# A gated feed-forward kernel: smaller first weight groups in separate buffer slots, a first chunk interleaved by input piece, and warmup matmuls

## The chip, the cores and the metric

The kernel runs on one core of a Trainium2 chip. The time is the device time of one execution in microseconds (us), 319.64 us for the kernel before: the median of 6 runs, which lie between 319.05 and 321.4 us. The profile comes from one more execution, of 319.37 us, whose span from the first to the last instruction is 317.6 us.

A core has five engines with their own instruction streams: TensorE (PE, matrix products; its weight loads are shown as PEld), VectorE (DVE), ScalarE (ACT), GpSimd (POOL) and SyncE (SP). They wait for each other on semaphores. Transfers between memory and the on-chip buffers run on 16 DMA engines; SyncE, ScalarE and GpSimd each issue them on a queue of their own (q1, q10 and q0 in the profile).

## What is computed

With x of 1024 rows (32 x 32) and 1024 columns, and weights in bf16:

```python
B, S, D, F = 32, 32, 1024, 3584
# x: (B, S, D), w_gate and w_up: (D, F), w_down: (F, D)
def reference(x, w_gate, w_up, w_down):
    return (_gelu(x @ w_gate) * (x @ w_up)) @ w_down
```

`_gelu` is the tanh approximation of GELU.

## The kernel before

**Tiling.** The hidden dimension F of 3584 is cut into 28 chunks of 128 (`FM = 28`, index m). The contraction over D = 1024 is cut into 8 slices of 128 (`DK`, index dk), the 1024 rows into two halves of 512 (`NH`, index h). For one chunk PE does 16 matmuls for the gate (called G) and 16 for the up projection (U), each 128x128 weights against 128x512 of x (L259). A chunk fills four PSUM banks of 512 columns: two for G, two for U; `s = m % 2` says which half of the eight banks. PE therefore works on one chunk while ScalarE and VectorE turn the other into a slice of `hT`: Square and Sigmoid on ScalarE (L304, L307), three operations on VectorE (L322, L327, L330), the last of which is D3. PE waits for D3 of chunk m - 2 before it starts chunk m. After all chunks a second stage (L279) multiplies `hT` by the down weights `wd`, 448 matmuls, and copies and stores the result.

**Input.** x must lie with its columns on the partitions. SyncE loads it with four DMA transposes (L212), one for each half of the rows (h) and half of the columns (q2): pieces (0,0), (0,1), (1,0), (1,1), each with a semaphore of its own. Slices dk 0 to 3 need q2 = 0, slices 4 to 7 need q2 = 1.

**Weights.** Gate and up weights come in groups of chunks. `gsizes` is 1, 3, and then 4 six times. Each of `wg` and `wu` has two buffers of 512 columns (four chunks), and group j goes to the start of buffer `j % 2`. Gate groups 0 and 1 are issued by ScalarE (L296), the later ones by SyncE (L223) behind the transposes; all up groups are issued by GpSimd (L200). The second group, on both engines, is held back until the second piece of x has landed:

```python
if j == 1:
    act.wait(Q_X[(0, 1)], ctx.get(("x", 0, 1)))
```

GpSimd has the same two lines. From group 2 on a load waits until PE has finished the first chunk of the group before (G of it on SyncE, U of it on GpSimd): then the buffer's old contents have been used. The down weights, seven groups of four chunks (`issue_wd`, L185), are issued between the others.

**Order on PE.** The order is written out by hand in `prog_pe`: chunk by chunk, in a chunk first all of G and then all of U, in each first h = 0 and then h = 1, with dk innermost. In chunk 0 each matmul waits for its piece of x. As all of G comes before U, the last four G matmuls of chunk 0 need piece (1,1), and the 16 U matmuls stand behind them. PE also waits for the group's gate and up loads before the first matmul of the group.

Of the kernel before, what the change touches and what calls it, by code (L numbers as in the profile page):

```python
# [6 lines left out]
P = 128  # L7
# [81 lines left out]
def bass_standalone__geglu_ffn__sampling_kernel(  # L89
# [13 lines left out]
    DK = D // P  # L103
# [3 lines left out]
    DH = D // 512  # L107
    assert NH == 2 and DH == 2 and DK == 8, "kernel specialised for N=1024, D=1024"

    gsizes = [1, 3]  # L110
    while sum(gsizes) < FM:
        gsizes.append(min(4, FM - sum(gsizes)))
    groups = []
    c = 0
    for gsz in gsizes:
        groups.append((c, gsz))
        c += gsz
    NG = len(groups)
    chunk_group = {}
    for j, (c0, gsz) in enumerate(groups):  # L120
        for i in range(gsz):
            chunk_group[c0 + i] = (j, i)
    NWB = 2

    WDG = 4
# [10 lines left out]
    C_DVE = _Clock("dve")  # L136
    C_POOL = _Clock("pool")
    Q_X = {(h, q2): _Clock(f"x{h}{q2}", 16) for h in range(2) for q2 in range(2)}
    Q_WGA = [_Clock("wga0", 16), _Clock("wga1", 16)]
    Q_WG = [_Clock("wg0", 16), _Clock("wg1", 16)]  # L140
    Q_WU = [_Clock("wu0", 16), _Clock("wu1", 16)]
    Q_WD_SP = _Clock("wd_sp", 16)
    Q_WD_POOL = _Clock("wd_pool", 16)
    Q_OUT = _Clock("out", 16)
    all_clocks = [C_PE, C_ACT, C_DVE, C_POOL, *Q_X.values(), *Q_WGA, *Q_WG, *Q_WU,
                  Q_WD_SP, Q_WD_POOL, Q_OUT]

    ctx = _Ctx()
# [1 line left out]
    with ExitStack() as es:  # L150
# [22 lines left out]
        def u_full(s):  # L173
            return ps[:, 4 * s + 2:4 * s + 4, :].rearrange("p a b -> p (a b)")

        def wslice(r, j):
            c0, gsz = groups[j]
            return r[:, :, c0 * P:(c0 + gsz) * P]

        def issue_wd(ew, eng, mine, upto_chunk, clock, force=False):  # L180
            for k in list(mine):
# [5 lines left out]

        def prog_pool(eng):
            pool = _Eng(ctx, eng, C_POOL)
            wd_mine = [k for k in range(len(wd_groups)) if k % 2 == 1]  # L190
            for j in range(NG):
                buf = j % NWB
                c0, gsz = groups[j]
                if j == 1:
                    pool.wait(Q_X[(0, 1)], ctx.get(("x", 0, 1)))
                if j >= NWB:
                    pc0, _pgsz = groups[j - 1]
                    pool.wait(C_PE, ctx.get(("U", pc0)))
                ctx.set(("wu", j), pool.do(
                    lambda: eng.dma_start(wu_bufs[buf][:, :, 0:gsz * P], wslice(wu_r, j)),  # L200
                    clock=Q_WU[buf]))
                if j >= NWB:
                    issue_wd(pool, eng, wd_mine, groups[j - 1][0], Q_WD_POOL)
            issue_wd(pool, eng, wd_mine, FM, Q_WD_POOL, force=True)
            ctx.set("wd_pool_total", Q_WD_POOL.n)

        def prog_sp(eng):
            sp = _Eng(ctx, eng, None)
            for h in range(NH):
                for q2 in range(2):  # L210
                    ctx.set(("x", h, q2), sp.do(
                        lambda: eng.dma_start_transpose(  # L212
                            xT[:, 4 * q2:4 * q2 + 4, h * 512:(h + 1) * 512],
                            xf[h * 512:(h + 1) * 512, q2 * 512:(q2 + 1) * 512],
                        ), clock=Q_X[(h, q2)]))
            wd_mine = [k for k in range(len(wd_groups)) if k % 2 == 0]
            for j in range(NWB, NG):
                buf = j % NWB
                c0, gsz = groups[j]
                pc0, _pgsz = groups[j - 1]  # L220
                sp.wait(C_PE, ctx.get(("G", pc0)))
                ctx.set(("wg", j), sp.do(
                    lambda: eng.dma_start(wg_bufs[buf][:, :, 0:gsz * P], wslice(wg_r, j)),  # L223
                    clock=Q_WG[buf]))
                issue_wd(sp, eng, wd_mine, pc0, Q_WD_SP)
            issue_wd(sp, eng, wd_mine, FM, Q_WD_SP, force=True)
            ctx.set("wd_sp_total", Q_WD_SP.n)
            last = None
            for tc in range(TC):
                for dh in range(DH):  # L230
                    sp.wait(C_ACT if dh == 0 else C_DVE, ctx.get(("E", tc, dh)))
                    last = sp.do(lambda: eng.dma_start(
                        out_r[:, tc, dh * 512:(dh + 1) * 512],
                        osb[:, tc, dh * 512:(dh + 1) * 512]), clock=Q_OUT)
            sp.wait(Q_OUT, last)

        def prog_pe(eng):
            pe = _Eng(ctx, eng, C_PE)
            for m in range(FM):
                j, fi = chunk_group[m]  # L240
                s = m % 2
                buf = j % NWB
                if fi == 0:
                    if j < NWB:
                        pe.wait(Q_WGA[j], ctx.get(("wg", j)))
                    else:
                        pe.wait(Q_WG[buf], ctx.get(("wg", j)))
                    pe.wait(Q_WU[buf], ctx.get(("wu", j)))
                if m >= 2:
                    pe.wait(C_DVE, ctx.get(("D3", m - 2)))  # L250
                for (key, wbufs, bank0) in (("G", wg_bufs, 4 * s), ("U", wu_bufs, 4 * s + 2)):
                    wb = wbufs[buf]
                    v = None
                    for h in range(NH):
                        for dk in range(DK):
                            if m == 0:
                                pe.wait(Q_X[(h, dk // 4)], ctx.get(("x", h, dk // 4)))
                            last = (dk == DK - 1 and h == NH - 1)
                            v = pe.do(lambda: eng.matmul(  # L259
                                ps[:, bank0 + h, :],  # L260
                                wb[:, dk, fi * P:(fi + 1) * P],
                                xT[:, dk, h * 512:(h + 1) * 512],
                                start=(dk == 0), stop=(dk == DK - 1),
                            ), mark=last)
                    ctx.set((key, m), v)
            pe.wait(C_DVE, ctx.get(("D3", FM - 2)))
            pe.wait(Q_WD_SP, ctx.get("wd_sp_total"))
            pe.wait(Q_WD_POOL, ctx.get("wd_pool_total"))
            for tc in range(TC):
                for dh in range(DH):  # L270
                    b = (tc % 4) * 2 + dh
                    if tc >= 4:
                        pe.wait(C_ACT if dh == 0 else C_DVE, ctx.get(("E", tc - 4, dh)))
                    v = None
                    for m in range(FM):
                        if m == FM - 1:
                            pe.wait(C_DVE, ctx.get(("D3", FM - 1)))
                        last = (m == FM - 1)
                        v = pe.do(lambda: eng.matmul(  # L279
                            ps[:, b, :],  # L280
                            hT[:, m, tc * P:(tc + 1) * P],
                            wd[:, m, dh * 512:(dh + 1) * 512],
                            start=(m == 0), stop=(m == FM - 1),
                        ), mark=last)
                    ctx.set(("O", tc, dh), v)

        def prog_act(eng):
            act = _Eng(ctx, eng, C_ACT)
            act.do(lambda: eng.activation(warm[:, 0:1], const0, ACTF.Sigmoid))  # L289
            for j in range(NWB):  # L290
                buf = j % NWB
                c0, gsz = groups[j]
                if j == 1:
                    act.wait(Q_X[(0, 1)], ctx.get(("x", 0, 1)))
                ctx.set(("wg", j), act.do(
                    lambda: eng.dma_start(wg_bufs[buf][:, :, 0:gsz * P], wslice(wg_r, j)),  # L296
                    clock=Q_WGA[j]))
            for m in range(FM):
                s = m % 2
                tb, ib = t_bufs[m % 2], i_bufs[m % 2]  # L300
                act.wait(C_PE, ctx.get(("G", m)))
                if m >= 2:
                    act.wait(C_DVE, ctx.get(("D2", m - 2)))
                ctx.set(("A1", m), act.do(lambda: eng.activation(  # L304
                    tb[:, :], g_full(s), ACTF.Square, scale=SQ_SCALE)))
                act.wait(C_DVE, ctx.get(("D1", m)))
                ctx.set(("A2", m), act.do(lambda: eng.activation(  # L307
                    tb[:, :], ib[:, :], ACTF.Sigmoid, scale=SIG_SCALE)))
            for tc in range(TC):
                dh = 0  # L310
                b = (tc % 4) * 2 + dh
                act.wait(C_PE, ctx.get(("O", tc, dh)))
                ctx.set(("E", tc, dh), act.do(lambda: eng.activation(  # L313
                    osb[:, tc, dh * 512:(dh + 1) * 512], ps[:, b, :], ACTF.Copy)))
# [74 lines left out]
```

## Time and profile before

| What | Value |
|---|---|
| Time, median of 6 | 319.64 us |
| Span of the profiled run | 317.6 us |
| PE busy | 294.6 us, 93% of the span, 1344 matmuls |
| DVE busy / ACT busy | 34% / 20% |
| First matmul of the kernel starts | 7.85 us |
| First matmul after the last piece of x starts | 24.96 us |
| Second stage starts | 217.99 us |
| Last matmul ends | 314.70 us |
| Landing of x pieces, from issue | 4.2 to 15.6 us |
| Landing of the 768 KB loads: wg / wu | 6.1 / 14.9 us from issue |

How to read it: an engine's busy share says how much of the whole span it worked, not what set the end. The chain of waits does that; it goes back from the last instruction to whatever released each step. Lines of the timeline give the start, the length, the engine, the line of the code, the operation with its output and inputs, and a count; in brackets the idle time before it and the work that ended that. A table of windows gives for each stretch the busy time and the number of instructions of PE, PEld, DVE, ACT and POOL, then the granted clock of TensorE (1.00 is full), the busy share of the DMA engines and the rate in GB/s. A DMA share above 100% means that packets of an engine overlapped in time.

### The profile page before, as it was taken

The page shows a single profiled execution, that of the slowest core. Times are in us where ns is not written, and L with a number is a line of the kernel's source. Part 1 is how long each engine was busy: PE and PEld are TensorE (multiplying, and loading weights), DVE is VectorE, ACT ScalarE, POOL GpSimd, SP SyncE. Part 2 cuts the span into 40 slices and gives each one's busy share as a digit, 9 for nine tenths or more (in the row PEclk, how much of TensorE's full clock was granted, in tenths as well). Part 3 has the DMA queues.
Part 4 walks back from the last instruction along what each step waited for, and adds up shares of the span by engine and source line. Part 5 has one row for each costly group of instructions (what it writes and reads, how often), then busy time and mean ns, then how long its engine had stood idle before and what let it go on. Part 6 is the DMA issues. An engine that isn't in the chain of part 4 may idle for free.

```text
span 317.6 us, 2954 instructions
## 1 busy us (share of the span) xinstructions
PE 294.6 (93%) x1344; PEld 131.9 (42%) x1344; DVE 108.1 (34%) x92; ACT 64.5 (20%) x66; POOL 9.7 (3%) x15
## 2 busy tenths in 40 slices
PE   0608999999999999999999999999999999999996
PEld 0103444444444444444444444444444444444442
DVE  0001554455555445455545545554000000000000
ACT  1002222323322232322233232222000000000000
POOL 1100100100010020000002000000000000000000
PEclk9956999999999999999999999999999999999999
DMA  8950440830380086047007700000010000001000
GB/s 169 252 106 1 130 137 0 290 108 0 107 289 2 0 294 236 1 125 274 0 0 255 277 0 0 2 0 0 17 35 17 17 27 25 17 17 35 17 17 33
DMA packets 23788, 26.40 MB, mean 83 GB/s; under 512 B 9968, under 2 KB 19184, under 8 KB 23776
## 3 DMA queue, kind: packets, MB, share of 16 engines
q1 hardware_dynamic: 18976, 14.68, 15.3%
q0 software_dynamic: 2720, 10.49, 10.5%
q10 hardware_dynamic: 2080, 1.05, 1.4%
q8 instruction: 10, 0.16, 0.2%
q14 instruction: 2, 0.02, 0.0%
HBM read 22.02 MB, written 2.10 MB: 76 GB/s over the span
## 4 chain that ended last, share of the span: by engine, by line
PE 91%; DMA 5%; SPq 3%; DVE 0%; issue 0%
PE ps L259 61%; PE ps L279 30%; DMA xT<-in_x_dram 5%; SPq L212 3%; DVE osb L336 0%
## 5 line engine op out<-in xcount | busy, mean ns | idle before, releaser
L259 PE MATMUL ps<-xT,wg 128*128 128x512 bf16 x448 | 104.5, 387 | 20.0 <-DMA xT<-in_x_dram 12.2
L259 PE MATMUL ps<-xT,wu 128*128 128x512 bf16 x448 | 102.5, 382 | 0.0
L279 PE MATMUL ps<-wd,hT 128*128 128x512 bf16 x448 | 96.9, 379 | 0.0
L259 PEld LDWEIGHTS ps<-xT,wg 128*128 128x128 bf16 x448 | 43.9, 99 | 75.2 <-DMA xT<-in_x_dram 14.3
L259 PEld LDWEIGHTS ps<-xT,wu 128*128 128x128 bf16 x448 | 44.1, 99 | 54.2 <-issue 2.2
L279 PEld LDWEIGHTS ps<-wd,hT 128*128 128x128 bf16 x448 | 43.8, 98 | 52.9
L322 DVE SCALAR_TENSOR_TENSOR ib<-tb,ps 128x1024 f32<-128x1024 f32 x28 | 34.2, 1221 | 80.9 <-ACT tb L304 80.9
L304 ACT ACTIVATE tb<-ps 128x1024 f32<-128x1024 f32 x28 | 28.6, 1023 | 121.4 <-PE ps L259 121.4
L327 DVE TENSOR_TENSOR sb<-tb,ps 128x1024 f32<-128x1024 f32 x28 | 34.2, 1221 | 36.1 <-PE ps L259 36.1
L307 ACT ACTIVATE tb<-ib 128x1024 f32<-128x1024 f32 x28 | 29.6, 1057 | 36.0 <-DVE ib L322 36.0
L336 DVE CAST osb<-ps 128x512 bf16<-128x512 f32 x8 | 5.5, 691 | 89.3 <-PE ps L279 89.3
L330 DVE TENSOR_TENSOR hT<-sb,ps 128x1024 bf16<-128x1024 f32 x28 | 34.2, 1220 | 1.0
L313 ACT ACTIVATE osb<-ps 128x512 bf16<-128x512 f32 x8 | 4.8, 597 | 86.6 <-PE ps L279 86.6
L200 POOL DMA_DIRECT2D wu<-in_w_up_dram x8 | 7.2, 903 | 161.7 <-PE ps L259 153.3
L185 POOL DMA_DIRECT2D wd<-in_w_down_dram x3 | 2.3, 760 | 0.0
L289 ACT ACT_TABLE_LOAD x1 | 1.3, 1283 | 0.7 <-PEq L374 0.7
L289 ACT ACTIVATE warm<-const-float32-0.0 128x1 f32<-128x1 f32 x1 | 0.2, 203 | 0.0
L374 POOL MEMSET const-float32-0.0<- 128x1 f32 x1 | 0.1, 98 | 0.2 <-issue 0.2
L374 POOL MEMSET const-bfloat16-1.0<- 128x1 bf16 x1 | 0.1, 101 | 0.0
L374 POOL MEMSET const-float32-1.0<- 128x1 f32 x1 | 0.1, 98 | 0.0
L374 POOL MEMSET const-uint8-127<- 128x1 uint8 x1 | 0.1, 98 | 0.0
## 6 DMA issues: line engine op xcount, KB each, us to landing
wg<-in_w_gate_dram SPq DMA_DIRECT2D x6, 1024.0 KB, 5.4
wu<-in_w_up_dram POOLq DMA_DIRECT2D x6, 1024.0 KB, 7.2
wd<-in_w_down_dram SPq DMA_DIRECT2D x4, 1024.0 KB, 7.7
wd<-in_w_down_dram POOLq DMA_DIRECT2D x3, 1024.0 KB, 8.3
out_dram<-osb SPq DMA_DIRECT2D x16, 128.0 KB, 1.7
wg<-in_w_gate_dram ACTq DMA_DIRECT2D x1, 768.0 KB, 6.1
wu<-in_w_up_dram POOLq DMA_DIRECT2D x1, 768.0 KB, 14.9
wg<-in_w_gate_dram ACTq DMA_DIRECT2D x1, 256.0 KB, 3.7
```

Of the source, the lines that this page charges most:

```text
L185: ew.do(lambda: eng.dma_start(wd[:, a:b, :], wd_r[:, a:b, :]), clock=clock)
L200: lambda: eng.dma_start(wu_bufs[buf][:, :, 0:gsz * P], wslice(wu_r, j)),
L212: lambda: eng.dma_start_transpose(xT[:, 4 * q2:4 * q2 + 4, h * 512:(h + 1) * 512], xf[h * 512:(h + 1) * 512, q2 * 512:(q2 + 1) * 512],), c ...
L259: v = pe.do(lambda: eng.matmul(ps[:, bank0 + h, :], wb[:, dk, fi * P:(fi + 1) * P], xT[:, dk, h * 512:(h + 1) * 512], start=(dk == 0), sto ...
L279: v = pe.do(lambda: eng.matmul(ps[:, b, :], hT[:, m, tc * P:(tc + 1) * P], wd[:, m, dh * 512:(dh + 1) * 512], start=(m == 0), stop=(m == F ...
L304: ctx.set(("A1", m), act.do(lambda: eng.activation(tb[:, :], g_full(s), ACTF.Square, scale=SQ_SCALE)))
L307: ctx.set(("A2", m), act.do(lambda: eng.activation(tb[:, :], ib[:, :], ACTF.Sigmoid, scale=SIG_SCALE)))
L313: ctx.set(("E", tc, dh), act.do(lambda: eng.activation(osb[:, tc, dh * 512:(dh + 1) * 512], ps[:, b, :], ACTF.Copy)))
L322: ctx.set(("D1", m), dve.do(lambda: eng.scalar_tensor_tensor(out=ib[:, :], in0=tb[:, :], scalar=1.0, in1=g_full(s), op0=ALU.add, op1=ALU.m ...
L327: ctx.set(("D2", m), dve.do(lambda: eng.tensor_tensor(sub[:, :], tb[:, :], u_full(s), ALU.mult)))
L330: ctx.set(("D3", m), dve.do(lambda: eng.tensor_tensor(hT[:, m, :], sub[:, :], g_full(s), ALU.mult)))
L336: ctx.set(("E", tc, dh), dve.do(lambda: eng.tensor_copy(osb[:, tc, dh * 512:(dh + 1) * 512], ps[:, b, :])))
```

## The change

There are three edits, all for the start of the kernel.

1. **Weight groups and slots.** The groups become 1, 1, 2, 3, then 4 five times and a last one of 1. Each group gets a buffer and a first slot in it; groups 2 and 3 are put beside groups 0 and 1 in the same buffers (slots from 1), so that they needn't wait for PE. What a later group must wait for is worked out from the slots' last users (`group_war`). Each group has semaphores of its own. Groups 0 and 1 are issued at once, without waiting for x. On GpSimd, group 2 waits for the second piece of x; SyncE issues gate groups 2 and 3 straight after the transposes. Loads are to be ready earlier.
2. **Chunk 0 by piece of x.** PE goes through chunk 0 in the order of the four pieces, and for each piece does four G and four U matmuls. All other chunks keep their order. More work is to be done as x comes in.
3. **Warmup.** GpSimd fills 128x512 elements of the output buffer with ones as its first instruction, and PE multiplies these eight times into a PSUM bank before its real work. This is to raise PE's clock early.

```diff
-    gsizes = [1, 3]
+    gsizes = [1, 1, 2, 3]
     while sum(gsizes) < FM:
         gsizes.append(min(4, FM - sum(gsizes)))
...
+    for j, gsz in enumerate(gsizes):
+        if j < 4:
+            buf, slot0 = (j % 2), (0 if j < 2 else 1)
+        else:
+            buf, slot0 = (j % 2), 0
+        groups.append((c, gsz, buf, slot0))
...
+    for j, (c0, gsz, buf, slot0) in enumerate(groups):
+        prev = [slot_owner.get((buf, sl)) for sl in range(slot0, slot0 + gsz)]
+        prev = [pp for pp in prev if pp is not None]
+        group_war.append(max(prev) if prev else None)
...
         def prog_pool(eng):
             pool = _Eng(ctx, eng, C_POOL)
+            ctx.set("scr", pool.do(lambda: eng.memset(osb[:, 0, 0:512], 1.0)))
...
-                if j == 1:
+                if j == 2:
                     pool.wait(Q_X[(0, 1)], ctx.get(("x", 0, 1)))
-                if j >= NWB:
-                    pc0, _pgsz = groups[j - 1]
-                    pool.wait(C_PE, ctx.get(("U", pc0)))
+                if group_war[j] is not None:
+                    pool.wait(C_PE, ctx.get(("U", group_war[j])))
...
         def prog_sp(eng):
...
-            for j in range(NWB, NG):
-                pc0, _pgsz = groups[j - 1]
-                sp.wait(C_PE, ctx.get(("G", pc0)))
+            for j in range(2, NG):
+                if group_war[j] is not None:
+                    sp.wait(C_PE, ctx.get(("U", group_war[j])))
...
+        NDUMMY = 8
+
         def prog_pe(eng):
             pe = _Eng(ctx, eng, C_PE)
+            pe.wait(C_POOL, ctx.get("scr"))
+            for i in range(NDUMMY):
+                v = pe.do(lambda: eng.matmul(ps[:, 7, :], osb[:, 0, 0:P], osb[:, 0, 0:512],
+                                             start=True, stop=True), mark=(i == NDUMMY - 1))
+            pe.wait(C_PE, v)
...
+                if m == 0:
+                    order = []
+                    for (h, q2) in XPIECES:
+                        for key in ("G", "U"):
+                            for dk in range(4 * q2, 4 * q2 + 4):
+                                order.append((key, h, dk))
...
         def prog_act(eng):
-            for j in range(NWB):
-                if j == 1:
-                    act.wait(Q_X[(0, 1)], ctx.get(("x", 0, 1)))
+            for j in range(2):
                 ctx.set(("wg", j), act.do(
```

More of the change, by code (lines that the diff above doesn't have):

```diff
@@ L114, in bass_standalone__geglu_ffn__sampling_kernel @@
     c = 0
-    for gsz in gsizes:
-        groups.append((c, gsz))
+    for j, gsz in enumerate(gsizes):
[3 more added lines that the diff above has]
+            buf, slot0 = (j % 2), 0
+        assert slot0 + gsz <= 4
+        groups.append((c, gsz, buf, slot0))
         c += gsz
     NG = len(groups)
-    chunk_group = {}
-    for j, (c0, gsz) in enumerate(groups):
+    chunk_info = {}
+    for j, (c0, gsz, buf, slot0) in enumerate(groups):
         for i in range(gsz):
-            chunk_group[c0 + i] = (j, i)
+            chunk_info[c0 + i] = (j, buf, slot0 + i)
+    group_war = []
+    slot_owner = {}
+    for j, (c0, gsz, buf, slot0) in enumerate(groups):
+        prev = [slot_owner.get((buf, sl)) for sl in range(slot0, slot0 + gsz)]
+        prev = [pp for pp in prev if pp is not None]
+        group_war.append(max(prev) if prev else None)
+        for sl in range(slot0, slot0 + gsz):
+            slot_owner[(buf, sl)] = c0 + gsz - 1
     NWB = 2
@@ L138, in bass_standalone__geglu_ffn__sampling_kernel @@
     Q_X = {(h, q2): _Clock(f"x{h}{q2}", 16) for h in range(2) for q2 in range(2)}
-    Q_WGA = [_Clock("wga0", 16), _Clock("wga1", 16)]
-    Q_WG = [_Clock("wg0", 16), _Clock("wg1", 16)]
-    Q_WU = [_Clock("wu0", 16), _Clock("wu1", 16)]
+    Q_WG = [_Clock(f"wg{j}", 16) for j in range(NG)]
+    Q_WU = [_Clock(f"wu{j}", 16) for j in range(NG)]
     Q_WD_SP = _Clock("wd_sp", 16)
@@ L144, in bass_standalone__geglu_ffn__sampling_kernel @@
     Q_OUT = _Clock("out", 16)
-    all_clocks = [C_PE, C_ACT, C_DVE, C_POOL, *Q_X.values(), *Q_WGA, *Q_WG, *Q_WU,
+    all_clocks = [C_PE, C_ACT, C_DVE, C_POOL, *Q_X.values(), *Q_WG, *Q_WU,
                   Q_WD_SP, Q_WD_POOL, Q_OUT]
@@ L174, in u_full, with wsrc, wdst @@
             return ps[:, 4 * s + 2:4 * s + 4, :].rearrange("p a b -> p (a b)")
-        def wslice(r, j):
-            c0, gsz = groups[j]
+        def wsrc(r, j):
+            c0, gsz, _buf, _slot0 = groups[j]
             return r[:, :, c0 * P:(c0 + gsz) * P]
+        def wdst(bufs, j):
+            _c0, gsz, buf, slot0 = groups[j]
+            return bufs[buf][:, :, slot0 * P:(slot0 + gsz) * P]
         def issue_wd(ew, eng, mine, upto_chunk, clock, force=False):
@@ L189, in prog_pool @@
             pool = _Eng(ctx, eng, C_POOL)
+            ctx.set("scr", pool.do(lambda: eng.memset(osb[:, 0, 0:512], 1.0)))
             wd_mine = [k for k in range(len(wd_groups)) if k % 2 == 1]
+            known_chunk = -1
             for j in range(NG):
-                buf = j % NWB
-                c0, gsz = groups[j]
-                if j == 1:
+                c0, gsz, buf, slot0 = groups[j]
+                if j == 2:
                     pool.wait(Q_X[(0, 1)], ctx.get(("x", 0, 1)))
-                if j >= NWB:
-                    pc0, _pgsz = groups[j - 1]
-                    pool.wait(C_PE, ctx.get(("U", pc0)))
+                if group_war[j] is not None:
+                    pool.wait(C_PE, ctx.get(("U", group_war[j])))
+                    known_chunk = max(known_chunk, group_war[j])
@@ L199, in prog_pool @@
                 ctx.set(("wu", j), pool.do(
[L200 to L203, printed above, removed]
+                    lambda: eng.dma_start(wdst(wu_bufs, j), wsrc(wu_r, j)),
+                    clock=Q_WU[j]))
+                if j >= 2:
+                    issue_wd(pool, eng, wd_mine, known_chunk, Q_WD_POOL)
@@ L204, in prog_pool @@
             issue_wd(pool, eng, wd_mine, FM, Q_WD_POOL, force=True)
             ctx.set("wd_pool_total", Q_WD_POOL.n)
+        XPIECES = [(0, 0), (0, 1), (1, 0), (1, 1)]
         def prog_sp(eng):
             sp = _Eng(ctx, eng, None)
[L209 to L215, printed above, removed]
@@ L216, in prog_sp @@
-            wd_mine = [k for k in range(len(wd_groups)) if k % 2 == 0]
-            for j in range(NWB, NG):
-                buf = j % NWB
-                c0, gsz = groups[j]
-                pc0, _pgsz = groups[j - 1]
-                sp.wait(C_PE, ctx.get(("G", pc0)))
+            for (h, q2) in XPIECES:
+                ctx.set(("x", h, q2), sp.do(
+                    lambda: eng.dma_start_transpose(
+                        xT[:, 4 * q2:4 * q2 + 4, h * 512:(h + 1) * 512],
+                        xf[h * 512:(h + 1) * 512, q2 * 512:(q2 + 1) * 512],
+                    ), clock=Q_X[(h, q2)]))
@@ L222, in prog_sp @@
+            wd_mine = [k for k in range(len(wd_groups)) if k % 2 == 0]
+            known_chunk = -1
+            for j in range(2, NG):
+                c0, gsz, buf, slot0 = groups[j]
+                if group_war[j] is not None:
+                    sp.wait(C_PE, ctx.get(("U", group_war[j])))
+                    known_chunk = max(known_chunk, group_war[j])
                 ctx.set(("wg", j), sp.do(
-                    lambda: eng.dma_start(wg_bufs[buf][:, :, 0:gsz * P], wslice(wg_r, j)),
-                    clock=Q_WG[buf]))
@@ L225, in prog_sp @@
-                issue_wd(sp, eng, wd_mine, pc0, Q_WD_SP)
+                    lambda: eng.dma_start(wdst(wg_bufs, j), wsrc(wg_r, j)),
+                    clock=Q_WG[j]))
+                issue_wd(sp, eng, wd_mine, known_chunk, Q_WD_SP)
             issue_wd(sp, eng, wd_mine, FM, Q_WD_SP, force=True)
@@ L235, in prog_sp @@
             sp.wait(Q_OUT, last)
+        NDUMMY = 8
         def prog_pe(eng):
             pe = _Eng(ctx, eng, C_PE)
+            pe.wait(C_POOL, ctx.get("scr"))
+            v = None
+            for i in range(NDUMMY):
+                v = pe.do(lambda: eng.matmul(ps[:, 7, :], osb[:, 0, 0:P], osb[:, 0, 0:512],
+                                             start=True, stop=True), mark=(i == NDUMMY - 1))
+            ctx.set("dummy", v)
+            pe.wait(C_PE, v)
             for m in range(FM):
-                j, fi = chunk_group[m]
+                j, buf, slot = chunk_info[m]
@@ L241, in prog_pe @@
                 s = m % 2
[L242 to L248, printed above, removed]
+                if m == groups[j][0]:
+                    pe.wait(Q_WG[j], ctx.get(("wg", j)))
+                    pe.wait(Q_WU[j], ctx.get(("wu", j)))
                 if m >= 2:
@@ L250, in prog_pe @@
                     pe.wait(C_DVE, ctx.get(("D3", m - 2)))
[L251 to L265, printed above, removed]
+                if m == 0:
+                    order = []
+                    for (h, q2) in XPIECES:
+                        for key in ("G", "U"):
+                            for dk in range(4 * q2, 4 * q2 + 4):
+                                order.append((key, h, dk))
+                else:
+                    order = [(key, h, dk) for key in ("G", "U") for h in range(NH)
+                             for dk in range(DK)]
@@ new lines, in prog_pe @@
+                cnt = {"G": 0, "U": 0}
+                for (key, h, dk) in order:
+                    wb = (wg_bufs if key == "G" else wu_bufs)[buf]
+                    bank = 4 * s + (0 if key == "G" else 2) + h
+                    if m == 0:
+                        pe.wait(Q_X[(h, dk // 4)], ctx.get(("x", h, dk // 4)))
+                    cnt[key] += 1
+                    last = (cnt[key] == NH * DK)
+                    v = pe.do(lambda: eng.matmul(
+                        ps[:, bank, :],
+                        wb[:, dk, slot * P:(slot + 1) * P],
+                        xT[:, dk, h * 512:(h + 1) * 512],
+                        start=(dk == 0), stop=(dk == DK - 1),
+                    ), mark=last)
+                    if last:
+                        ctx.set((key, m), v)
@@ L289, in prog_act @@
             act.do(lambda: eng.activation(warm[:, 0:1], const0, ACTF.Sigmoid))
-            for j in range(NWB):
-                buf = j % NWB
-                c0, gsz = groups[j]
-                if j == 1:
-                    act.wait(Q_X[(0, 1)], ctx.get(("x", 0, 1)))
+            for j in range(2):
                 ctx.set(("wg", j), act.do(
-                    lambda: eng.dma_start(wg_bufs[buf][:, :, 0:gsz * P], wslice(wg_r, j)),
-                    clock=Q_WGA[j]))
+                    lambda: eng.dma_start(wdst(wg_bufs, j), wsrc(wg_r, j)),
+                    clock=Q_WG[j]))
             for m in range(FM):
```

## The prediction

> **What bounds the kernel now.** I read the chain of waits first. It shows which work set the end.
>
> ```profile
> 7.24 2.07 SPq L212
> 9.31 0.04 issue
> 9.35 15.56 DMA xT<-in_x_dram
> 24.91 0.05 issue
> 24.96 193.03 PE ps L259 x884
> 217.99 96.71 PE ps L279 x448
> 314.70 0.02 issue
> 314.72 0.69 DVE osb L336
> ```
>
> From 24.96 us on TensorE (PE) never stops: 884 matmuls of the first stage, then 448 of the second. Everything before is the arrival of x, whose fourth transpose takes 15.56 us from issue to landing. So only two things can move the time: when PE begins its unbroken run, and how many matmuls are left then. The PE timeline of the start comes next (start, length, count, idle time before it and what ended it).
>
> ```profile
> 7.85 4.93 PE L259 MATMUL ps<-xT,wg 128*128 128x512 bf16 x12 [7.85 <-DMA wu<-in_w_up_dram]
> ...
> 24.96 1.89 PE L259 MATMUL ps<-xT,wg 128*128 128x512 bf16 x4 [12.17 <-DMA xT<-in_x_dram]
> ...
> 26.64 4.87 PE L259 MATMUL ps<-xT,wu 128*128 128x512 bf16 x16
> ...
> 31.35 1.03 PE L259 MATMUL ps<-xT,wg 128*128 128x512 bf16 x4
> ```
>
> PE did 12 matmuls as the first three pieces of x came, idled 12.17 us, and then had 20 matmuls of chunk 0 left. These took 31.35 - 24.96 = 6.39 us. The steady spacing is (217.99 - 31.35)/864 = 0.216 us, so 20 would take 4.32 us: 2.1 us are lost to a slow clock, which the table of windows shows (PEclk is third from the end).
>
> ```profile
> 16.00:18.00 2.00, 0.00 (x0) 0.00 (x0) 0.00 (x0) 0.00 (x0) 0.00 (x0) 0.50 0.72 51
> ...
> 26.00:28.00 2.00, 2.00 (x6) 0.67 (x5) 0.06 (x1) 1.02 (x1) 0.00 (x0) 0.50 0.00 0
> ```
>
> Why is the fourth piece late? The DMA view by stretch (packets, MB, share of the 16 engines) tells. First 8 to 10 us, then 12 to 14, then 16 to 25; q1 is SyncE's queue, q10 ScalarE's, q0 GpSimd's.
>
> ```profile
> q1 hardware_dynamic: 2080, 0.52, 116.7%
> ```
> ```profile
> q10 hardware_dynamic: 635, 0.49, 83.6%
> q1 hardware_dynamic: 374, 0.10, 25.8%
> ```
> ```profile
> q0 software_dynamic: 175, 0.71, 37.8%
> q1 hardware_dynamic: 540, 0.13, 11.8%
> ```
>
> Alone, x moves one whole piece (2080 packets, 0.52 MB) in 2 us. From 12 to 14 us the 768 KB of wg hold the engines, and no x packet at all moves from 11 to 12. From 16 us the last 540 x packets trickle for 8 us beside the 768 KB of wu on q0. Both loads were released by the second piece (9.5 us). At its own rate the fourth piece would have ended about 2 us after the third, which landed at 7.24 + 4.2 = 11.4 us.
>
> **What the Trainium skill says.** "DMA: Bandwidth & Descriptors", section Queues, rings and completion order: each DMA engine takes the queues in turn, a whole packet at a time. The trace agrees: a q0 packet holds 0.71 MB/175 = 4.1 KB, an x packet 0.25 KB, so x waits out a packet 16 times its size at each turn. The same page, Specifications, gives about 1 us to the first byte of a GpSimd DMA; here it is longer: wu was issued at 9.80 us and q0 shows no packet before 15 us. I use the measurement. "TensorE: Matmul & The Clock Gate", Part 1: the array runs at half clock until it has been busy for a window of about 3.4 us, and falls back after an idle one. The trace agrees: weight loads started 0.42 us apart at 7.8 us, and the clock was at half from about 15.5 us (work had ended at 12.8) to 29.2 us.
>
> **The change part by part.**
> *Groups of 1, 1, 2, 3 chunks.* Before, 1.05 MB of weights competed with the fourth piece from 10.9 us on. Now 0.26 MB of wg and of wu move ahead of it, to the very start, and ScalarE issues nothing at 9.5 us. SyncE's wg for chunks 2 to 6 (1.31 MB) stand behind the fourth transpose in the same queue. GpSimd's wu for chunks 2 to 6 (1.31 MB) are still released by the second piece.
> Cost at the start: by 4 us 0.33 MB had moved. The first piece (0.52 MB) and four loads of 0.26 MB are 1.57 MB; the other 1.24 MB at 240 GB/s (mean of 4 to 12 us) take 5.2 us, plus 0.5 us from last packet to landing (third piece: last packet before 11 us, landed 11.4). That is 9.7 us if all drain first; wu of chunk 1 need not. From below: 7.85 us, if nothing shifts. I take S = 9.4 us for the start of real matmuls, close to the upper end since the packets take turns.
> The fourth piece: all of x and the four loads are 2.10 + 1.05 = 3.15 MB; (3.15 - 0.33)/0.24 = 11.8 us after 4 us, plus 0.5: T = 16.3 us. The second piece lands about two pieces of 2.05 us earlier than T, at some 12 us; wu issued then shows packets 4 to 5 us later (issued at 1.26, first seen after 5 us; at 9.80, after 15), at 16 us or more. The fourth piece should just slip past it.
> *Interleaving.* Each x piece now feeds 8 matmuls, gate and up. Before T there are 24 instead of 12, so 8 remain instead of 20: 12 x 0.216 = 2.6 us off the path if T binds. From S, with a cold start, 24 matmuls take 10 x 0.427 + 14 x 0.216 = 7.3 us (0.427 is the cold spacing of the TensorE page, Part 1; the trace showed 0.42) and end at 16.7 us, after T. So PE runs through from S. ScalarE gets chunk 0 a little later relative to PE's restart; the chain of ScalarE and VectorE is 1.0 + 1.2 + 1.1 + 1.2 + 1.2 = 5.7 us, under the 6.9 us of chunk 1, so chunk 2 does not wait for it.
> *Warmup.* One MEMSET of 128x512, then 8 matmuls. The trace has only 128x1 (0.1 us). "GPSIMD Engine Reference", section Elementwise — side-by-side cycle accounting, gives 769 ns for 512 elements in a one-input loop; no run here shows it. Between 0.1 and 0.8 us I take 0.8: wu of chunk 0, behind it on GpSimd, goes from 7.8 to 8.6 us, still before S. The 8 matmuls are 8 x 0.427 = 3.4 us, from about 2 to 5.5 us, on an idle PE: no cost. Gain between 0 and 2.1 us (the cold loss); I take 0, since 3.9 us of idleness follow, and 2.7 us (12.8 to 15.5) were enough to lose the clock before.
> *Slots, semaphores, later waits.* wg now waits for an U instead of a G, and the load of chunks 7 to 10 for U of chunk 3: three chunks of 6.9 us, 20.7 us ahead, against landings of 5 to 7 us. The last down weights are issued after chunk 22, five chunks early. Cost nothing: PE's own matmuls hide these loads.
> *Sum.* S + 896 x 0.216 (193.5) + 448 (96.7) + cold loss 2.1 + from last matmul to end 2.9 (317.6 - 314.70) + outside the span 2.0 (319.64 - 317.6) = S + 297.2 = **306.6 us**. If T binds instead, 872 first-stage matmuls remain: T + 188.4 + 96.7 + 2.1 + 2.9 + 2.0 = T + 292.1. The same sum for the kernel before, with 884 and 24.96, gives 319.6.
>
> **The rivals.**
> *A, as above*, 306.6. Within it chunk 2 could wait for its wu: issued at 12 us and landing 14.9 us later as its forerunner did, 26.9, against a start at 9.4 + 2.1 + 64 x 0.216 = 25.3: 1.6 us more, 308.2.
> *B, the tail is caught.* Everything slips by a few us at the start, q0 arrives while a part of the fourth piece is under way, T = 20: 312.1. For it: the margin above is under 1 us. Against: x ran at full rate beside wu of chunk 0 at 5 us.
> *C, a new load takes the place of the old.* q0 holds the fourth piece as it does now, T = 25: 317.1.
> *D, slower.* 1.31 MB on q0 instead of 0.79 MB, at the 0.71 MB in 8 us of the trickle, from 15 us: 14.8 us, T = 30.3, 322.4. For it: more bytes on exactly the queue beside which x crawled. Against: that queue starts late, and ScalarE's load, which let it catch up, is gone.
>
> **How the numbers follow.** A 0.58, B 0.22, C 0.10, D 0.10. Faster by over 0.5% means below 318.0: A, B and most of C, 0.87. Same 0.04 and slower 0.09 come from the rest of C and from D. Range: from 303.0 (S = 7.85 with the clock kept warm: 7.85 + 297.2 - 2.1) up to 317.0, which takes in B and the early half of C; D and the late half of C are left out.
>
> **What would show it.** Right: the fourth transpose lands within 8 us of issue, the PE's longest idle time after its first real matmul is under 2 us, no q0 packets in numbers before that landing, and the chain of waits begins PE's run near 9.4 us. Interleaving: x4 groups alternate wg and wu. Warmup: eight matmuls done by 6 us, and half the clock again at S. Wrong: a gap of many us ended by xT with q0 busy in it (B to D), or one ended by wu at chunk 2.

## The result, and the profile after

The changed kernel takes 314.37 us (median of 20 runs, 309.9 to 318.13), beside 319.45 us for the kernel before on the same chips (median of 40 runs, 314.73 to 325.62). The ratio is 0.983 (95% interval 0.979 to 0.987): 1.7% faster, some 5.5 us at the old time. Ratios, here and below, leave out the executions more than 1.5% above the fastest one of the same kernel, so they can differ from the ratio of the medians. 306.6 us had been forecast, so only some 5 of the expected 13 us came. The profiled run took 314.82 us, close to the median; its span is 313.0 us.

The chain of waits of the changed kernel, from the third piece of x on (start, length, what):

```profile
9.89 1.89 SPq L230
11.78 0.04 issue
11.82 10.39 DMA xT<-in_x_dram
22.21 0.05 issue
22.26 191.22 PE ps L292 x872
213.48 96.71 PE ps L313 x448
```

It has the same shape as before. PE's unbroken run still begins when the fourth piece of x lands, at 22.26 instead of 24.96 us, and 872 instead of 884 matmuls of the first stage remain. The piece is issued 2.5 us later than before and takes 10.4 us instead of 15.6 us to land.

The PE timeline of the start (start, length, count; in brackets the idle time and what ended it):

```profile
1.32 3.28 PE L263 MATMUL ps<-osb 128*128 128x512 bf16 x8 [1.32 <-POOL osb L206]
...
9.43 1.87 PE L292 MATMUL ps<-xT,wg 128*128 128x512 bf16 x4 [4.83 <-DMA wu<-in_w_up_dram]
...
16.18 1.03 PE L292 MATMUL ps<-xT,wu 128*128 128x512 bf16 x4
...
22.26 1.89 PE L292 MATMUL ps<-xT,wg 128*128 128x512 bf16 x4 [5.05 <-DMA xT<-in_x_dram]
```

Real work starts at 9.43 us, the 24 matmuls end at 17.2 us, and then PE waits 5.05 us for the last piece. The clock is gone again by then. In the table of windows (TensorE clock third from the end, then DMA share and GB/s):

```profile
16.00:18.00 2.00, 1.21 (x6) 0.36 (x4) 0.00 (x0) 0.00 (x0) 0.00 (x0) 1.00 1.28 123
...
22.00:24.00 2.00, 1.74 (x5) 0.64 (x6) 0.00 (x0) 0.00 (x0) 0.00 (x0) 0.50 1.11 286
```

In the DMA view by stretch one sees the fourth piece being caught. Packets, MB and share, first for 14 to 15 us, then 15 to 16, then 18 to 20; q1 is SyncE's queue, q0 GpSimd's:

```profile
q1 hardware_dynamic: 907, 0.23, 158.0%
q0 software_dynamic: 3, 0.01, 12.9%
```
```profile
q1 hardware_dynamic: 41, 0.01, 77.2%
q0 software_dynamic: 7, 0.03, 12.6%
```
```profile
q0 software_dynamic: 166, 0.65, 104.9%
q1 hardware_dynamic: 30, 0.01, 2.0%
```

Each piece has 2080 packets. By 15 us the queue has moved 7570, that is 1330 of the fourth piece. In the next microsecond, as the first q0 packets show, it moves 41 instead of about 1000. q0 itself moves only 7 then, so the two queues together carry 0.04 MB, where x alone carried 0.28 MB from 13 to 14 us. The stall thus begins before q0's own bytes fill the engines; why both queues stand still there is not shown. By 18 us 2031 are through; the last 49 need until 22 us, while q0 moves 278 packets of 4 KB. The prediction had the data through at 15.8 us. It was less than 1 us short, and that cost 6 us.

### The profile page after: what moved, and what is told of

The parts are those of the page before. It is cut to its first block, busy times and chain, and to the rows that moved or that the text cites. A ratio compares the mean times of both kernels' runs of the same rounds, so it can differ in the third digit from the quotient of the medians.

```text
span 313.0 us, 2978 instructions
## 1 busy us (share of the span) xinstructions
PE 299.0 (96%) x1352; PEld 133.6 (43%) x1352; DVE 108.1 (35%) x92; ACT 64.5 (21%) x66; POOL 11.9 (4%) x18
## 3 DMA queue, kind: packets, MB, share of 16 engines
q10 hardware_dynamic: 2080, 0.52, 0.7%
## 4 chain that ended last, share of the span: by engine, by line
PE 92%; SPq 3%; DMA 3%; DVE 0%; issue 0%
PE ps L292 61%; PE ps L313 31%; SPq L230 3%; DMA xT<-in_x_dram 3%; DVE osb L366 0%
## 5 line engine op out<-in xcount | busy, mean ns | idle before, releaser
L217 POOL DMA_DIRECT2D wu<-in_w_up_dram x10 | 9.0, 898 | 167.6 <-PE ps L292 158.6
L263 PE MATMUL ps<-osb 128*128 128x512 bf16 x8 | 3.3, 586 | 1.3 <-POOL osb L206 1.3
L263 PEld LDWEIGHTS ps<-osb 128*128 128x128 bf16 x8 | 1.0, 141 | 3.0 <-issue 1.7
```

Of the source, the lines that this page charges most:

```text
L217: lambda: eng.dma_start(wdst(wu_bufs, j), wsrc(wu_r, j)),
L263: v = pe.do(lambda: eng.matmul(ps[:, 7, :], osb[:, 0, 0:P], osb[:, 0, 0:512], start=True, stop=True), mark=(i == NDUMMY - 1))
```

## The experiments

Each kernel was compared with the kernel before on the same chip. Ratios are to that kernel; they are the safer figures across the rows, since the median of the kernel before was itself between 318.0 and 320.3 us in the different comparisons.

| Kernel | Median us | Ratio (95% interval) |
|---|---|---|
| The change | 314.37 | 0.983 (0.979 to 0.987) |
| The change, up loads held | 306.49 | 0.967 (0.964 to 0.971) |
| The change, gate loads held | 314.09 | 0.989 (0.986 to 0.993) |
| The change, both held | 306.57 | 0.967 (0.964 to 0.971) |
| The change, up loads by ScalarE | 313.85 | 0.990 (0.987 to 0.994) |
| The change without warmup | 314.14 | 0.988 (0.980 to 0.996) |
| The change without interleaving | 316.46 | 0.995 (0.992 to 0.998) |
| Before, with interleaving alone | 316.53 | 0.993 (0.989 to 0.996) |
| Before, second group held | 310.42 | 0.976 (0.972 to 0.980) |
| Loads by need | 305.16 | 0.963 (0.960 to 0.967) |
| Loads by need, 16 warmup matmuls | 304.66 | 0.959 (0.955 to 0.963) |

### Which load catches the fourth piece?

Up loads held: on GpSimd, group 2 waits for the fourth piece instead of the second.

```diff
                 if j == 2:
-                    pool.wait(Q_X[(0, 1)], ctx.get(("x", 0, 1)))
+                    pool.wait(Q_X[(1, 1)], ctx.get(("x", 1, 1)))
```

> The changed kernel, with GpSimd's up loads for chunks 2 to 6 released by the fourth piece of x instead of the second. Theory 1 (the arrival of these loads on q0 stalls the fourth piece): the fourth piece lands at 16 to 17 us instead of 22.2, PE runs through from 9.4 us, time 306 to 309 us. Theory 2 (the gate loads that SyncE issues right behind the fourth piece on its own queue stall it): no change, 314 us, landing near 22 us. Theory 3 (the early loads already make the piece late): landing at 20 us or later, 312 to 314 us.

Measured: 306.49 us (306.32 to 306.98). The fourth piece, issued at 12.0 us, lands 4.5 us later. From 14 to 16 us q1 has all the engines, and no q0 packet is there:

```profile
q1 hardware_dynamic: 1808, 0.46, 111.3%
```

The PE timeline of this run has no gap any more at the piece, and none at chunk 2, for which the up load is now issued at 16.79 us:

```profile
15.76 1.03 PE L292 MATMUL ps<-xT,wu 128*128 128x512 bf16 x4
16.62 1.03 PE L292 MATMUL ps<-xT,wg 128*128 128x512 bf16 x4
...
25.25 3.62 PE L292 MATMUL ps<-xT,wg 128*128 128x512 bf16 x16
```

Gate loads held: SyncE waits for the fourth piece before it issues its gate loads.

```diff
             for j in range(2, NG):
                 c0, gsz, buf, slot0 = groups[j]
+                if j == 2:
+                    sp.wait(Q_X[(1, 1)], ctx.get(("x", 1, 1)))
```

> The changed kernel, with SyncE's gate loads for chunks 2 to 6 held until the fourth piece of x has landed; the up loads as in the change. Theory 1: no change, 314 us, landing near 22 us with the x packets stalled when the first q0 packets show. Theory 2: landing at 16 to 17 us, 306 to 309 us. Theory 3: 312 to 314 us.

Measured: 314.09 us; in its profile the fourth piece lands at 21.5 us. Not much changes: the loads behind the piece on its own queue are not what holds it.

This run also shows how little has to be left over for the piece to be caught. GpSimd issued at 12.49 us, and q0's first packets came after 15.7 us. SyncE's queue held nothing but x then, and from 0 to 16 us it moved:

```profile
q1 hardware_dynamic: 8244, 2.09, 65.4%
```

All of x is 4 x 2080 = 8320 packets. Only 76 were left, about a tenth of what was left in the changed kernel, and still the piece landed 5.5 us later.

> Both loads held until the fourth piece has landed. Theory 1 and theory 2: landing at 16 us, PE runs through from 9.4 us to the end of chunk 1 at about 25.3 us; the weights of chunk 2, issued at 16.3 us, must land by then or PE waits for them (8 to 10 us after issue: up to 1 us of waiting); 306 to 308 us. Theory 3: landing after 20 us, 312 us or more.

Both edits together: 306.57 us, the same as the first alone. Of the three theories, these runs fit only the first. The run-to-run spread goes too: 8 us in the change and with the gate loads held (20 and 22 runs), under 1 us in the two that keep the up loads away (6 runs each).

### Is it GpSimd's queue, or any load?

The up loads for chunks 2 to 6 go to ScalarE, on the old release; GpSimd skips them.

```diff
...
+            act.wait(Q_X[(0, 1)], ctx.get(("x", 0, 1)))
+            for j in (2, 3):
+                ctx.set(("wu", j), act.do(
+                    lambda: eng.dma_start(wdst(wu_bufs, j), wsrc(wu_r, j)),
+                    clock=Q_WU[j]))
```

> The changed kernel, with the up loads for chunks 2 to 6 issued by ScalarE (q10) instead of GpSimd (q0), on the same release by the second piece. Theory 1a (what stalls the fourth piece is the mixing of q0's traffic with a transpose): the piece lands at 16.5 to 18.5 us, 307 to 310 us. Theory 1b (any 1.31 MB of weights released there stands in the way): ScalarE's queue starts sooner than q0, within 2 us of issue, so the piece lands at 19 to 22 us, 311 to 314 us.

Measured: 313.85 us, with the fourth piece landing at 22.75 us: theory 1b. The DMA view from 14 to 16 us, now with ScalarE's q10:

```profile
q10 hardware_dynamic: 764, 0.39, 82.4%
q1 hardware_dynamic: 156, 0.04, 15.4%
```

The load itself stands in the way, whichever queue brings it. ScalarE's begins sooner after issue (some packets before 14 us, from an issue at 12.04), and holds the piece earlier. Nor does it take packets of 4 KB: ScalarE's hold about 0.5 KB each (0.39 MB in 764), and the piece is no earlier.

### What do the parts of the change bring?

Without the memset and the eight matmuls:

> The changed kernel without the memset and the eight warmup matmuls. If the warmup neither costs nor gives anything (as predicted): 314 us within 0.5%, real matmuls starting up to 0.5 us earlier, and 24 matmuls done long before the fourth piece in both. Rival (the warmup pays by keeping the clock up): 316 us, the 2.1 us of a cold start added. Rival (it costs, by delaying the first up load): 312 to 313 us.

Measured: 314.14 us. The intervals of the ratio overlap with those of the change, but they are too wide to exclude a gain of 2 us. The timeline settles it:

```profile
9.75 1.87 PE L284 MATMUL ps<-xT,wg 128*128 128x512 bf16 x4 [9.75 <-DMA wu<-in_w_up_dram]
```

Real work starts at 9.75 us, and its first four matmuls take 1.87 us, exactly as in the change: both start at the slow spacing. (The clock column reads 1.00 at this point of this run although the matmuls are slow, so the spacing is the safer sign.) The memset took 0.52 us and delayed nothing: GpSimd's first load went out at 1.29 us with it and at 1.25 us without. As put here, the warmup neither costs nor gives anything that these runs can show.

Chunk 0 in the old order (`if m < 0` in place of `if m == 0` at the new order):

> The changed kernel with chunk 0 in the old order (all of G, then all of U). The fourth piece binds PE at 22.3 us; 20 instead of 8 matmuls of chunk 0 remain then. Main theory: 12 x 0.216 = 2.6 us more, 317.0 us. Rival (the interleaving is worth nothing): 314.4 us.

Measured: 316.46 us. The medians are 2.1 us apart from the change; by the ratios it is 1.2%, 3.8 us. The two were compared with different executions of the kernel before, and with the intervals some 2 to 5 us are possible. Its fourth piece landed at 23.2 us in the profile, and 20 matmuls of chunk 0 followed it.

The other way round, the kernel before with only the new order of chunk 0:

```diff
+                if m == 0:
+                    order = [(key, h, dk) for h in range(NH) for q2 in range(2)
+                             for key in ("G", "U") for dk in range(4 * q2, 4 * q2 + 4)]
...
```

> The kernel before with only the interleaving of chunk 0. Main theory: 2.6 us less than before, 317 us against 319.6, that is half of the change's 5.1 us; the other half would then be the earlier landing of the fourth piece (22.3 instead of 25.0 us). Rival: no change.

Measured: ratio 0.993 (0.989 to 0.996), so 2.4 us with an interval of 1.3 to 3.5 us; 2.6 had been worked out. Grouping and warmup without interleaving bring 0.5% (0.2% to 0.8%), 1.7 us. So interleaving gave about as much as everything else in the change; with the intervals as they are, no more can be said of the halves.

The kernel before with only the release of its second group moved, the same edit on GpSimd and ScalarE:

```diff
                 if j == 1:
-                    pool.wait(Q_X[(0, 1)], ctx.get(("x", 0, 1)))
+                    pool.wait(Q_X[(1, 1)], ctx.get(("x", 1, 1)))
```

> The kernel before, with the second group's loads (768 KB each on ScalarE and GpSimd) released by the fourth piece of x instead of the second. Main theory: the fourth piece lands near 14 us instead of 25; chunk 0 ends at 18 us; PE then waits for wu of chunk 1, which takes 8 us or more from issue at 14 us: about 22 us, with a cold start after it: 22 + 864 x 0.216 + 2.1 + 96.7 + 4.9 = 312.3 us. Rival (the wait only changes its name): 318 to 320 us.

Measured: 310.42 us, 2.4% less than before: this one edit gains at least as much as the whole change. A new wait takes the place of the old one, as expected, but a short one. The PE timeline:

```profile
14.15 1.04 PE L259 MATMUL ps<-xT,wg 128*128 128x512 bf16 x4 [0.20 <-DMA xT<-in_x_dram]
15.03 3.62 PE L259 MATMUL ps<-xT,wu 128*128 128x512 bf16 x16
21.35 3.61 PE L259 MATMUL ps<-xT,wg 128*128 128x512 bf16 x16 [2.70 <-DMA wu<-in_w_up_dram]
```

The fourth piece lands at 14.1 us; chunk 1 then waits 2.70 us for its up weights. They came 6.81 us after issue, so chunk 1 began at 21.35 us where I had put 22 us, and PE kept its clock over the short wait, which spares the 2.1 us of a cold start. The profiled run (309.35 us) is 3.0 us better than expected, and these two account for 2.8 of them; the median is 1.9 us better.

### A version in the order of need

ScalarE issues gate and up of chunk 0. SyncE issues the four transposes and behind them gate and up of groups 1 to 3. GpSimd starts with group 4, after PE has done chunk 3.

```diff
         def prog_sp(eng):
-            for j in range(2, NG):
+            for j in range(1, NG):
...
                     clock=Q_WG[j]))
+                if j < 4:
+                    ctx.set(("wu", j), sp.do(
+                        lambda: eng.dma_start(wdst(wu_bufs, j), wsrc(wu_r, j)),
+                        clock=Q_WU[j]))
```

> The changed kernel with the loads of the start in the order of need: ScalarE issues gate and up of chunk 0 at once; SyncE issues gate and up of chunks 1 to 6 behind the four transposes on its own queue; GpSimd loads from chunk 7 on only. Interleaving and warmup as in the change. Theory 1 (nothing but GpSimd's load stalls the fourth piece, and loads behind it on its queue do not): first real matmul near 7.8 us, fourth piece near 14 us, PE runs through, 7.8 + 297.2 = 305.0 us. Rival (loads right behind the transposes slow them, or chunk 1's weights come too late, later than 7.8 + 2.1 + 6.9 = 16.8 us): 307 us or more with PE waiting for wg or wu of chunk 1.

Measured: 305.16 us; 3.7% less than before. Its PE timeline starts earlier and goes on:

```profile
7.85 1.86 PE L294 MATMUL ps<-xT,wg 128*128 128x512 bf16 x4 [2.93 <-DMA wu<-in_w_up_dram]
...
14.36 1.03 PE L294 MATMUL ps<-xT,wg 128*128 128x512 bf16 x4
15.22 1.03 PE L294 MATMUL ps<-xT,wu 128*128 128x512 bf16 x4
16.35 3.61 PE L294 MATMUL ps<-xT,wg 128*128 128x512 bf16 x15
```

The queue is used as a line: what is needed first is issued first, and loads behind the transposes do not slow them. Only 0.3 us is lost at chunk 1.

The same with `NDUMMY = 16`:

> The kernel with the loads by need, with 16 warmup matmuls instead of 8, so that they reach to about 6 us or later and less than 2 us of idleness lie before the first real matmul at 7.85 us. If a warmup pays once it reaches the real work: real matmuls start warm, the end is set by the fourth piece, near 13.5 us: 13.5 + 290.0 = 303.5 us. Rival (the clock falls back all the same, or the warmup runs into the real work): 305.2 us or more.

Measured: 304.66 us. The ratio's interval overlaps that of the kernel above, so a gain isn't shown. The clock did stay up:

```profile
1.32 5.93 PE L265 MATMUL ps<-osb 128*128 128x512 bf16 x16 [1.32 <-POOL osb L206]
8.39 1.02 PE L294 MATMUL ps<-xT,wg 128*128 128x512 bf16 x4 [1.15 <-DMA wu<-in_w_up_dram]
...
14.92 1.03 PE L294 MATMUL ps<-xT,wu 128*128 128x512 bf16 x4
16.96 3.61 PE L294 MATMUL ps<-xT,wg 128*128 128x512 bf16 x15 [1.01 <-DMA wu<-in_w_up_dram]
```

Four matmuls take 1.02 us from the first one on, not 1.86. But PE, now faster, arrives at chunk 1 before its up weights and waits 1.01 us. My expectation had set the end by the fourth piece and forgotten the load behind it.

## Why the prediction was wrong, point by point

**The bound, right.** The end is when PE's unbroken run begins plus what remains. The sum T + 292.1 gives 314.4 us for T = 22.26, the T of the profiled run; that run took 314.82 us. The difference of 0.5 us is small: the first stage took 191.22 us where 188.4 + 2.1 were put, and the ends a little less than put. That the median of all runs is 314.37 is a closer fit than the sum can claim.

**T, wrong: the step that failed.** "The fourth piece should just slip past it", T = 16.3 us. It was 22.26 us. The piece's own pace was right: with the up loads held it landed at 16.5 us. The release was right too (the second piece was to land at 12 us; GpSimd issued at 12.19). What failed was the time from issue to the first q0 packets: 4 to 5 us were taken from two loads of the kernel before; here they showed in the stretch from 14 to 15 us, about 2 to 3 us after issue. So the load arrived while 750 of 2080 packets were still to go. Even 3.2 us would not have been enough: that is what it was with the gate loads held, 76 packets were left, and T was 21.5 us. That B was the likelier case could have been read off the margin, which was under 1 us; I gave B 0.22. T lies between B (20) and C (25), and the cause is the one that B and C name: the released load holds the piece.

**Two readings of the kernel before, tested.** I read its late piece as held by the two 768 KB loads. Moving only their release brought the landing from 25 to 14.1 us: shown. The 1.05 MB of weights that I let compete with the fourth piece are too few: two loads of 768 KB are 1.57 MB, though no sum uses this. Against rival B I argued that x had run at full rate beside the up load of chunk 0; the trace has 740 x packets from 5 to 6 us, when q0 came in, after 1044 in the microsecond before, so this was no argument against B. Against rival D I argued that ScalarE's load, which had let q0 catch the piece, would be gone, as if only a pair of loads could do it. One load is enough. And the same load on ScalarE's queue holds the piece just as long: it is the load, not the queue. The Trainium skill's "DMA: Bandwidth & Descriptors", section Issuing engines are not separate DMA queues, says that transfers from all engines interleave on the same DMA engines, and these runs agree. But that x waits out one larger packet at each turn, as I reasoned, does not explain the trickle. From 16 to 25 us 540 x packets moved beside 175 of q0, three to one, and both together kept the engines busy only half of the time (11.8% and 37.8%). And ScalarE's packets of 0.5 KB held the piece as long as 4 KB packets. That the load holds the piece is shown; how it does so stays open.

**S, right in size, not in its releaser.** Real work starts at 9.43 us; 9.4 was worked out. That the two agree so well is in part luck: PE waited last for the up load of chunk 0, which I had put at 8.6 us, and not for x. With that load on ScalarE, and chunk 1's behind the transposes, it started at 7.85 us.

**Interleaving, right.** 2.6 us were worked out; it brought 2.4 us alone (1.3 to 3.5), and as the difference between with and without 2.1 us by the medians or 3.8 us by the ratios. These agree with 2.6 us but do not measure it closely. The count behind it is shown: 8 matmuls of chunk 0 follow the fourth piece instead of 20.

**Warmup, right.** Neither cost nor gain: the clock was at half when real work began (0.50 in the windows from 8 to 14 us), and the first four matmuls take 1.87 us with the warmup and without it. The memset took 0.52 us, between the two bounds, and less than the 0.8 us taken.

**Slots and later waits, right.** After the last piece nothing but matmuls is on the chain of waits: 191.22 us for 872 matmuls and 96.71 us for 448.

**The rivals.** D (slower, T = 30) did not come: the q0 load moved faster here (0.65 MB from 18 to 20 us) than the 0.71 MB in 8 us taken from the kernel before. What the forecast called A is what one gets with one line altered, the later release: real work from 9.64 us without a gap, and 306.49 us for 306.6.

## What to carry to other kernels

When a slow chain of small transfers sets the start, ask of every load in flight beside it what would happen if it came a microsecond earlier; if the answer is a stall, tie its release to the last small transfer, or queue it behind on the same queue. A margin smaller than the spread of a DMA's start is no margin, and it does not help to be nearly through: 76 packets left over cost nearly as much as 750. A wide spread between runs can be the sign of such a collision: 8 us in the changed kernel, 1 us once GpSimd's load was out of the way (with the load on ScalarE's queue the piece was late, but steadily so: 313.25 to 314.74 us).

## What the runs showed of the hardware that I had not expected

A transpose is held to its last packets: 49 of 2080 packets took 4 us beside 4 KB packets on another queue, and with the gate loads held 76 packets took over 5 us. The time from a GpSimd load's issue to its first packets isn't fixed: 2 to 3 us here, over 3 us with the gate loads held, over 4 us in the kernel before. And the issue of a transpose is no fixed cost either: with two more loads of 0.26 MB at the start, the second one's took 7.61 us in the changed kernel, against 4.96 us before; the cause was not tested.
